# Gated attention and MLP at decode: the Tile kernel rewritten with its own semaphores, and TensorE's rounds 0 to 11 as three loops

## The chip, the cores and the metric

The kernel runs on one core of one Trainium2 chip. A core has five engines that run side by side, each with an instruction stream of its own: TensorE (PE, matrix products; its weight loads are listed as PEld), VectorE (DVE), ScalarE (ACT), GpSimd (POOL) and SyncE (SP, which here only issues transfers). [...] Sixteen DMA engines carry data between HBM and the on-chip memory (SBUF); every transfer is cut into packets that are shared out among them. Matrix products land in PSUM, eight banks of 128 partitions by 512 float32 values.

The metric is the device time of one execution in microseconds (us). Before the change it is 680.88 us, the median of three runs (680.88 to 681.34).

## The reference

One token for each of two sequences (B = 2, D = 448) goes through an attention block with a cache (16 heads, 4096 cached positions, 256 values a head) and through a small MLP (F = 1792); a gate mixes the two. All is float32.

```
q      = (x @ wq) split into 16 heads of 256
scores = q . k_cache / 16          # 2 x 16 x 4096
p      = softmax(scores)
a      = (p . v_cache) @ wo
r      = max(x @ w1 + b1, 0)
b      = (r * r) @ w2 + b2
g      = sigmoid(sum(x * gate_w))
out    = g * a + (1 - g) * b       # 2 x 1 x 448
```

`k_cache` and `v_cache` have 2 x 16 x 4096 x 256 float32 values each, 134.2 MB each. Every one of them is read once.

## The kernel before

**Rounds.** The work goes in 16 rounds. Round i is one pair of heads of one sequence: `rounds[i] = (b, n)`, heads 2n and 2n+1, b alternating. A round has a K tile and a V tile, each 128 partitions by 64 rows of 256 values (8.4 MB): partitions 0 to 63 hold one head's 4096 positions, 64 to 127 the other's. There are three such buffers: `kp[0]` and `kp[1]` for K in even and odd rounds, and one, `vp`, for V.

**What a round does.** DVE multiplies the K tile in place by the query (`times_q`, line 282, in two halves) and sums each row (`row_sums`, line 288), which gives the scores. The maximum over partitions goes over PE: DVE reduces (`m`, line 292), PE spreads the column with the identity into `mt` (line 296), DVE reduces again (`nb`, line 302). ACT writes the exponentials as a weight tile `pw` for PE (line 307) with the row sums in `rs`. PE then runs `values` (line 333): 32 products of 16 weight columns by 512 values of V, which accumulate in a PSUM bank, `po_buf`. The 16 columns stand for the 8 (head, sequence) pairs of a group of four heads, so that a group's four rounds add into the same bank; columns that are not this round's have to be zero. Two weight tiles, `pw0` and `pw1`, are used in turn (by b), and DVE clears one with a memset where a tile passes to other columns (line 434). Two banks, `po_buf0` and `po_buf1`, are used in turn by group.

**The end of a group.** Rounds 0 to 3, 4 to 7 and 8 to 11 are the wide groups. After the fourth round's `softmax`, `sums` (line 313, PE) and `norm` (lines 319 to 322, DVE) give the normalised, gated reciprocals `rl`. After its `values`, `take_turn` transposes the accumulated bank: ACT copies it in four pieces into `shared` (line 350), PE multiplies them with `rl` into `ot` (line 355, 16 products), ACT copies `ot` to `oT` (line 360). The group's `wo` block (1.8 MB) is loaded into `kp[0]` once DVE has finished the first half of the next round's K there (`load_wo`, line 112), and `project` (line 374, 8 products of 448 columns) adds the group's output to `acc`. Only then may the K tile of a later round overwrite `kp[0]`. Rounds 12 to 15 form two narrow groups and the end: V of round 14 goes into a K buffer, V of round 15 comes in five parts, `wo` and `w2` follow, and `late` (line 379) adds all to `fin`.

**Loads.** All large transfers are issued by SP on one queue, in the order of the program: `wq`, K0, `w1`, K1, then V and K in turn: V(i), K(i+2). Each waits for the buffer to be free: V(i+1) for `values` of round i on PE, K(i+2) for the `row_sums` of round i on DVE, and the K after a group also for `project` on PE. The queue takes an issue before the one ahead has landed, so a load that is issued early enough leaves the DMA engines no gap.

**What sets the order.** Each engine runs its instructions in the order in which the code writes them (the Tile context schedules nothing). Tile adds the semaphores, a PSUM or SBUF buffer for each name, and at its end a wait for everything and two barriers over all engines.

## Time and profile before

| | |
|---|---|
| median of three runs | 680.88 us (680.88 to 681.34) |
| span of the profiled execution, first to last instruction | 678.9 us |
| what the median has beside that span | 2.0 us |
| bytes read from HBM | 289.56 MB, 427 GB/s over the span |
| DVE busy | 573.2 us (84%) |
| PE busy | 245.9 us (36%) |
| ACT busy | 35.5 us (5%) |

The profiled execution's time outside its span isn't listed; the 2.0 us are the difference between the median and the span. "Busy" is the time in which an engine had an instruction in work; register, branch and semaphore instructions are not counted. A line such as "DVE kp L282 <- DMA kp<-in_A_k_cache_dram: 53.2" says that DVE stood idle ahead of its line 282 for 53.2 us in all, until a transfer of K landed. "DMA share" in a table of windows is the mean busy share of the sixteen DMA engines in that stretch (packets that overlap an edge can push it over 1). The rows that carry the argument stand in the prediction.

### The profile page before, as it was taken

The numbers are of one execution on the slowest core, as the hardware profiler recorded it, in microseconds if no ns is written. First come the engines' busy times: TensorE is split into PE (matmuls) and PEld (weight loads), VectorE is DVE, ScalarE is ACT, GpSimd is POOL, SyncE is SP. The second block draws the span as 40 slices with busy tenths as digits, with TensorE's granted clock in tenths as the row PEclk, the third lists the DMA queues.
The fourth block names the chain that finished last, engine by engine and source line by source line (L and its number), as shares of the span: only waits on it lengthen the run. The fifth ranks groups of instructions, "written<-read, shape, count | busy, mean of one in ns | idle before, by whom it ended". The sixth has DMA issues, their size and how long they took to land.

```text
span 678.9 us, 3814 instructions
## 1 busy us (share of the span) xinstructions
PE 245.9 (36%) x1658; PEld 78.9 (12%) x1658; DVE 573.2 (84%) x150; ACT 35.5 (5%) x116; POOL 0.7 (0%) x6
## 2 busy tenths in 40 slices
PE   2522250503308541240515644050512550602476
PEld 1100210100104110010101301010100310100122
DVE  3069999999899995979989895998989799999920
ACT  0001000000001000000000100000000200100000
POOL 0000000000000000000000000000000000000000
PEclk9956575665757656575856578575655775755789
DMA  9999999999999999999999999999999999999996
GB/s 379 440 421 441 440 430 444 432 440 437 429 436 407 452 432 432 432 433 432 432 430 432 436 432 433 432 437 432 432 432 432 412 458 413 426 456 432 399 423 267
DMA packets 7628, 289.80 MB, mean 427 GB/s; under 512 B 950, under 2 KB 1084, under 8 KB 2364
## 3 DMA queue, kind: packets, MB, share of 16 engines
q1 hardware_dynamic: 7448, 289.54, 98.9%
q8 instruction: 13, 0.21, 0.1%
q10 hardware_dynamic: 164, 0.02, 0.0%
q14 instruction: 3, 0.02, 0.0%
HBM read 289.56 MB, written 0.00 MB: 427 GB/s over the span
## 4 chain that ended last, share of the span: by engine, by line
DVE 47%; DMA 44%; issue 6%; PE 3%; ACT 0%; SPq 0%; DVEq 0%; ACTq 0%
DMA kp<-in_A_k_cache_dram 32%; DVE kp L282 25%; DVE s L288 21%; DMA vp<-in_A_v_cache_dram 9%; DMA kp<-in_B_w_dram 2%; PE po_buf L333 2%; PE mt L296 0%; DVE pw L434 0%; PE fin L379 0%; ACT pw L307 0%; DVE m L292 0%; PE sum L313 0%; DVE nb L302 0%; SPq L77 0%; DVE hb L270 0%
## 5 line engine op out<-in xcount | busy, mean ns | idle before, releaser
L282 DVE TENSOR_TENSOR kp<-kp,q 128x8192 f32<-128x8192 f32 (+2 forms) x34 | 278.2, 8182 | 53.2 <-DMA kp<-in_A_k_cache_dram 53.2
L288 DVE TENSOR_REDUCE s<-kp 128x32 f32<-128x8192 f32 x32 | 277.9, 8686 | 1.1
L333 PE MATMUL po_buf<-vp,pw 128*16 128x512 f32 (+1 forms) x960 | 140.9, 747 | 219.1 <-DMA vp<-in_A_v_cache_dram 219.1
L333 PEld LDWEIGHTS po_buf<-vp,pw 128*16 128x16 f32 (+1 forms) x960 | 31.0, 112 | 324.2 <-issue 248.3
L296 PE MATMUL mt<-ident,m 128*64 128x64 f32 x64 | 7.3, 317 | 138.9 <-DVE m L292 138.9
L374 PE MATMUL acc<-kp,oT 128*2 128x448 f32 x48 | 26.8, 730 | 18.8 <-issue 18.8
L307 ACT ACTIVATE pw<-s,nb 64x64 f32<-64x64 f32 x32 | 11.1, 347 | 388.6 <-DVE nb L302 388.4
L296 PEld LDWEIGHTS mt<-ident,m 128*64 128x64 f32 x64 | 4.8, 192 | 149.6 <-issue 127.6
L355 PE MATMUL ot<-rl,shared 128*128 128x8 f32 x96 | 17.0, 307 | 3.8 <-ACT shared L350 3.4
L355 PEld LDWEIGHTS ot<-rl,shared 128*128 128x128 f32 x96 | 16.1, 253 | 7.2 <-ACT shared L350 7.2
L238 PE MATMUL pq<-qs,ident 128*64 128x256 f32 x64 | 14.1, 529 | 0.7 <-ACT qs L226 0.7
L200 PE MATMUL ph<-vp,xT 128*4 128x448 f32 x28 | 7.2, 679 | 17.3 <-DMA vp<-in_B_w_dram 17.3
L333 PE MATMUL po_buf<-kp,pw 128*8 128x512 f32 x64 | 9.6, 752 | 8.7 <-DMA kp<-in_A_v_cache_dram 8.7
L302 DVE TENSOR_REDUCE nb<-mt 128x1 f32<-128x64 f32 x16 | 3.6, 224 | 10.7 <-PE mt L296 10.7
L350 ACT ACTIVATE shared<-po_buf 128x512 f32<-128x512 f32 x12 | 6.5, 594 | 86.5 <-PE po_buf L333 81.1
L200 PE MATMUL po_buf<-vp,xT 128*4 128x512 f32 x56 | 7.8, 714 | 4.9 <-DMA vp<-in_A_wq_dram 4.9
L241 ACT ACTIVATE q<-pq 128x256 f32<-128x256 f32 x16 | 6.1, 383 | 62.5 <-PE pq L238 62.3
L374 PEld LDWEIGHTS acc<-kp,oT 128*2 128x2 f32 x48 | 4.8, 103 | 38.9 <-issue 38.9
L319 DVE RECIPROCAL rc<-sum 128x8 f32<-128x8 f32 (+1 forms) x5 | 1.0, 196 | 9.2 <-PE sum L313 9.2
L307 ACT ACTIVATION_READ_ACCUMULATOR pw<-s,nb 64x1 f32 x32 | 5.9, 184 | 0.0
L434 DVE MEMSET pw<- 128x512 f32 x10 | 4.8, 485 | 0.6
L238 PEld LDWEIGHTS pq<-qs,ident 128*64 128x64 f32 x64 | 4.4, 176 | 4.2 <-issue 2.3
(61 smaller groups left out, 58.1 us busy)
## 6 DMA issues: line engine op xcount, KB each, us to landing
kp<-in_A_k_cache_dram SPq DMA_DIRECT2D x4, 4096.0 KB, 27.6
vp<-in_A_wq_dram SPq DMA_DIRECT2D x1, 7168.0 KB, 19.5
kp<-in_A_wo_dram SPq DMA_DIRECT2D x4, 1792.0 KB, 25.5
vp<-in_A_v_cache_dram SPq DMA_DIRECT2D x1, 4096.0 KB
vp<-in_B_w_dram SPq DMA_DIRECT2D x1, 3136.0 KB
vp<-in_A_v_cache_dram SPq DMA_DIRECT2D x1, 2048.0 KB, 30.7
kp<-in_B_w_dram SPq DMA_DIRECT2D x2, 896.0 KB, 27.4
vp<-in_A_v_cache_dram SPq DMA_DIRECT2D x1, 1024.0 KB
```

Of the source, the lines that this page charges most:

```text
L200: nc.tensor.matmul(out[32 * g:32 * g + 2 * B, :width], xT[:, half, c].rearrange("p s b -> p (s b)"), t[:, (a * n + g) * width:(a * n + g + ...
L238: nc.tensor.matmul(pq[k * PH:(k + 1) * PH, :DH], ident[:, r:r + 1].to_broadcast([P, PH]), qs[:, k * DH:(k + 1) * DH], start=True, stop=True)
L241: nc.scalar.activation(q_sb[i], pq[:, :DH], AF.Copy)
L282: nc.vector.tensor_tensor(kt, kt, q_sb[i].unsqueeze(1).to_broadcast([P, hi - lo, DH]), op=ALU.mult)
L288: nc.vector.tensor_reduce(s_t[i][:, at], rows(kp[i % 2])[:, at, :], axis=AX.X, op=ALU.add)
L296: nc.tensor.matmul(mt[at, :PH], m.to_broadcast([P, PH]), ident[:, at], start=True, stop=True)
L307: nc.scalar.activation(pw[b][at, :, 2 * c:2 * c + 2], s_t[i][at].rearrange("p (m s) -> p m s", s=2), AF.Exp, bias=nb[at], accum_out=rs_t[u ...
L333: nc.tensor.matmul(po[r:r + 4 * n, :], pw[b][:, m, :4 * n], vt[:, 2 * m:2 * m + 2, :].rearrange("p j d -> p (j d)"), start=(k == 0 and b = ...
L350: nc.scalar.activation(o_w[:, s], pv[:, s, lo:lo + nj // 2].unsqueeze(2).to_broadcast([P, nj // 2, HG, HP]), AF.Copy)
L355: nc.tensor.matmul(ptv[:, lo + j, :], ov[:, s, j, :], rl_t[u][:, :, s], start=(s == 0), stop=(s == 1))
L374: nc.tensor.matmul(acc[:, :D], oT[g][:, j, :], wo_sb[g][:, j, :], start=False, stop=(g == NG - 2 and j == HJ - 1))
L434: nc.vector.memset(pw[b], 0.0)
```

## The change

The kernel is written without Tile. A small recorder, `Flow`, takes every operation with the regions that it reads and writes, works out which waits are needed, and emits each engine's stream with one semaphore for each engine and one for each transfer's buffer. The arithmetic, the tiles' sizes, the transfers and their order on SP stay.

- PE's rounds 0 to 11 are three loops of four passes (`flow.loop`, `next_pass`, `end_loop`, emitted with `nc.Fori`). The loop's body is `values`, then `mt`, then `pq`, the query of a later round. A looped instruction can't wait for a count that differs from pass to pass, so three hand-overs are tokens: the waiting engine waits for a semaphore's fixed value and takes it off again (`pw` from ACT, `v` from the DMA, `m` from DVE, and `q` from ACT). [...]
- All passes have to name the same operands. So there is one weight tile (`pw0`) and one bank (`po0`) for rounds 0 to 11. After each `values`, ACT overwrites the round's columns with zeros (`clear`), in place of DVE's memsets; after the first and second group ACT zeroes the bank, and every product is issued without a start flag. ACT also copies a column of the identity into `sel` (`pick`) so that `pq` can read the same operand in each pass; the query of round i+3 is made after `mt` of round i+1.
- `sums`, `norm`, the transposition (`turn_wide`) and `project` of a group all stand behind the group's loop on PE, that is, after `mt` of the following round. Before, `sums` and the transposition stood ahead of that `mt`.
- `mt`, `pq` and `sm` have one PSUM bank each.
- At the end SP waits for the two output transfers and clears the semaphores. There is no wait or barrier of the other engines.

TensorE at the end of the first group and in the next round, before the change (line 333 is `values`, 355 the transposition, 374 `project`):

```order
L333 MATMUL po_buf0_85<-vp_71,pw1_94 16x512 x32
L355 MATMUL ot0_446<-rl0_407,shared_135 128x8 x16
L296 MATMUL mt4_482<-ident_78,m4_480 64x64 x2
L374 MATMUL acc_89<-kp0_69,oT0_467 2x448 x8
L238 MATMUL pq6_498<-qs_130,ident_78 64x256 x2
L333 MATMUL po_buf1_87<-vp_71,pw0_92 16x512 x32
```

The same place now; all products have the line of one helper (332), the lines 161 are the loop's own, and the rows from the first `po0` to `COMPARE_AND_BRANCH` run four times:

```order
L161 ISA
L161 UNCONDITIONAL_BRANCH
L332 MATMUL po0<-vp,pw0 16x512 x32
L332 MATMUL mt<-ident,m 64x64 x2
L332 MATMUL pq<-qs,sel 64x256 x2
L161 REGISTER_ALU
L161 COMPARE_AND_BRANCH
L332 MATMUL sm<-rs0,ones_pp 128x8
L332 MATMUL sm<-rl0,shared 128x8 x16
L332 MATMUL acc<-kp0,oTw 2x448 x8
```

The transposition (`sm<-rl0,shared`) has moved from ahead of the next round's `mt` to behind it, directly ahead of `project`, and `sums` (`sm<-rs0,ones_pp`) has come with it.

SP's end before (line 98 loads `w2`, line 500 writes half of the output):

```order
L98 DMA kp_70<-in_B_w_dram 128x896
L98 DMA kp_70<-in_B_w_dram 128x1792 x2
L98 DMA kp_70<-in_B_w_dram 128x1344
L98 DMA kp_70<-in_B_w_dram 128x448
L500 DMA out_dram<-shared 4x112
L524 UNCONDITIONAL_BRANCH
```

And now:

```order
L253 DMA kp<-in_B_w_dram 128x896
L253 DMA kp<-in_B_w_dram 128x1792 x2
L253 DMA kp<-in_B_w_dram 128x1344
L253 DMA kp<-in_B_w_dram 128x448
L253 DMA out_dram<-shared 4x112
L168 ISA
```

The loads stand as before; the branch to Tile's closing block, with its barriers, has become one clearing of the semaphores.

The diff, cut to its core:

```diff
+class Flow:
...
+    def op(self, eng, fn, r=(), w=(), give=None, take=(), dma=None):
...
+        for t in take:
+            p = self.tokens[t].pop(0)
+            o.takes.append((t, 16 if p.proc not in self.eng else 1))
+            self.learn(know, p)
...
+        def one(o):
+            e = self.eng[o.eng]
+            for t, n in o.takes:
+                e.wait_ge(sem(t), n).then_inc(sem(t), -n)
+            for p in o.waits:
+                e.wait_ge(sem(p.proc), counts[id(p)])
+            i = o.fn()
...
+                    passes, body, slot = o
+                    with nc.Fori(0, passes, engines=bass.OrderedEngineSet([TYPES[PE]]),
+                                 head_slot=None if slot is None else {TYPES[PE]: slot}):
+                        for p in body:
+                            one(p)
+            if eng == SP:
...
+                nc.sync.sem_clear(range(nums[0], nums[0] + len(nums)))
...
+    def pick(i):
+        c = col(i)
+        op(ACT, lambda: s_.activation(sel, c, AF.Copy), r=["ident"], w=["sel"], give="q")
...
+    def clear(i):
+        b, n = rounds[i]
+        u, k = unit_of[2 * n]
+        at = pwt[0].rearrange("p m (k b s) -> p m k b s", b=B, s=2)[:, :, k:k + 2, b, :]
+        op(ACT, lambda: s_.activation(at, zero.unsqueeze(2).unsqueeze(3).to_broadcast([P, NK // 2, 2, 2]), AF.Copy), r=["zero"],
...
+    def turn_wide(u):
...
+        if u < NG - 2:
+            op(ACT, lambda: s_.activation(po, zero.to_broadcast([P, 512]), AF.Copy), r=["zero"], w=["po0"])
...
-    for i, (b, n) in enumerate(rounds[:-4]):
...
-        vt = load_v(i, vp)
-        mt = maximum(i)
-        softmax(i, mt)
-        if done:
-            norm(u, sums(u))
...
-        if group is not None:
-            project(group)
...
-        load_k(i + 2)
-        make_q(i + 2)
-        values(i, vt)
-        if done:
-            take_turn(u)
-        rest(i + 1, 0, 0)
...
-                nc.vector.memset(pw[b], 0.0)
-        if done:
-            load_wo(u, i + 1)
-            group = u
+    for i in range(LOOPED):
+        if i % HG == 0:
+            flow.loop()
+        flow.next_pass()
         vt = load_v(i, vp)
+        if i < last - 3 - 1 or i + 2 < 14:
+            load_k(i + 2)
         values(i, vt)
+        clear(i)
         rest(i + 1, 0, 0)
...
+        if i % HG == HG - 1:
+            load_wo(i // HG, i + 1)
+        maximum(i + 1, True)
+        softmax(i + 1)
+        make_q(i + 3, True)
+        if i < LOOPED - 1:
+            pick(i + 4)
+        if i % HG == HG - 1:
+            u = i // HG
+            flow.end_loop(16 * u)
+            sums(u)
+            norm(u)
+            turn_wide(u)
+            project(u)
...
-    nc.sync.dma_start(ov[0], y4[0:P:32, :])
-    nc.scalar.dma_start(ov[1], y4[1:P:32, :])
+    load(SP, "out0", ov[0], y4[0:P:32, :], ["out0"], r=[("shared", 0, DQ)])
+    load(ACT, "out1", ov[1], y4[1:P:32, :], ["out1"], r=[("shared", 0, DQ)])
+    op(SP, lambda: nc.sync.nop(), r=["out0", "out1"])
+    flow.emit()
```

## The prediction

> **What bounds the kernel now.** I read the page from the top: the engines' shares, the DMA rows, the chain, then windows, waits and timelines of the places that the change touches.

> ```profile
> span 678.9 us, 3814 instructions
> PE 245.9 (36%) x1658; PEld 78.9 (12%) x1658; DVE 573.2 (84%) x150; ACT 35.5 (5%) x116; POOL 0.7 (0%) x6
> q1 hardware_dynamic: 7448, 289.54, 98.9%
> q8 instruction: 13, 0.21, 0.1%
> DVE 47%; DMA 44%; issue 6%; PE 3%; ACT 0%; SPq 0%; DVEq 0%; ACTq 0%
> ```

> The chain of waits names DVE first, and DVE is busy for 84%. That misleads. The load queue q1 fills 98.9% of the time of sixteen DMA engines, and a table of windows shows that this has no weak stage:

> ```profile
> core 0: us, PE busy (x) PEld busy (x) DVE busy (x) ACT busy (x) POOL busy (x), PEclk, DMA share, GB/s
> 40.00:640.00 600.00, 206.71 (x1264) 65.63 (x1264) 558.88 (x123) 30.74 (x104) 0.00 (x0) 0.62 1.00 433
> 0.00:40.00 40.00, 12.91 (x76) 4.26 (x76) 5.71 (x23) 2.85 (x5) 0.70 (x6) 0.92 0.97 413
> ```

> From 40 to 640 us the share is 1.00 at 433 GB/s, 27 GB/s for each of the sixteen. The 289.54 MB of q1 at that rate are 668.7 us of the 678.9. DVE's chain runs inside this: a DVE that ends sooner issues the next K sooner, behind loads that are queued already. So the span is the head until the first byte, 668.7 us of transfer, whatever unbalances the sixteen engines, and the tail. In the middle the change can only lose, by letting the queue run dry.

> How the transfers end is seen in windows of half a microsecond:

> ```profile
> 671.00:671.50 0.50, 0.50 (x32) 0.50 (x24) 0.00 (x0) 0.00 (x0) 0.00 (x0) 1.00 1.01 409
> 671.50:672.00 0.50, 0.50 (x31) 0.50 (x26) 0.00 (x0) 0.00 (x0) 0.00 (x0) 1.00 0.82 333
> 672.00:672.50 0.50, 0.46 (x20) 0.19 (x9) 0.00 (x0) 0.00 (x0) 0.00 (x0) 1.00 0.60 240
> 672.50:673.00 0.50, 0.00 (x0) 0.00 (x0) 0.00 (x0) 0.00 (x0) 0.00 (x0) 1.00 0.50 201
> 673.00:673.50 0.50, 0.48 (x21) 0.48 (x25) 0.00 (x0) 0.00 (x0) 0.00 (x0) 1.00 0.43 172
> 673.50:674.00 0.50, 0.47 (x20) 0.20 (x9) 0.00 (x0) 0.00 (x0) 0.00 (x0) 1.00 0.23 93
> 674.00:674.50 0.50, 0.00 (x0) 0.00 (x0) 0.00 (x0) 0.00 (x0) 0.00 (x0) 1.00 0.37 122
> 674.50:675.00 0.50, 0.35 (x16) 0.35 (x20) 0.00 (x0) 0.00 (x0) 0.00 (x0) 1.00 0.05 18
> ```

> The share doesn't drop at once. The first of the sixteen engines are done at 671.5, half of them by 672.5, the last near 674.6, though all had the same bytes of q1. The seven shares from 671.5 on add up to 3.00, times 0.5 us: evenly spread, the work would have ended at 673.0. Something has held some engines back by up to 3.1 us. The candidate is q8: thirteen packets of instructions. 0.21 MB over thirteen is 16 KB each, and over the 3316 instructions of PE and PEld (2 x 1658) 64 bytes each, so q8 is TensorE's code. Its 0.1% (0.05 to 0.15 before rounding) of 16 x 678.9 us is 5.4 to 16.3 us, or 0.42 to 1.25 us a packet, of one engine each time. Thirteen packets can't be even over sixteen engines; an engine that carried two or three of them is late by about what is seen.

> The tail behind the last load, and the closing rows of Tile (line 524):

> ```profile
> 674.65 0.99 PE fin L379 x32
> 675.72 0.26 ACT shared L498
> 676.01 0.65 SPq L500 DMA_DIRECT2D out_dram<-shared  x1
> L524 SPq DRAIN  x3: 7/7/7, 678.2 to 678.5; - x3
> L524 SPq EVENT_SEMAPHORE  x7: 17/28/28, 676.7 to 678.8; - x7
> L524 POOLq EVENT_SEMAPHORE_RANGE_CLEAR  x1: 96/96/96, 678.5 to 678.5; - x1
> ```

> The output is issued at 676.01 and has landed when SP's first drain stands at 678.2; from there to 678.9 are two barriers and a clearing of semaphores.

> **The change part by part.** The sum is made against the profiled span, 678.9, and the 2.0 us by which the median of the runs (680.88) exceeds it are carried over unchanged.

> *End without barriers.* Removed: what lies between 678.2 and 678.9, 0.7 us. Added: SP's own clearing, 0.1 us by the 96 ns row, while five fewer semaphore waits at 28 ns and more are ahead of it, so these cancel. All of it is on the path. Term: -0.7 us (bounds -0.5 and -0.8).

> *Shorter TensorE code.* The program calls 505 products where there were 829, and four instructions stand for each (3316 over 829): 2020 of 64 bytes, 8 packets in place of 13, if a pass through a loop doesn't load its code again. Five packets fewer are 0.1 to 0.4 us on the mean engine, but the end is set by the worst one. If that loses one packet of 1.25 us, the last load lands 1.2 us sooner. Bounds: 0, if the late engines keep their packets; and -2.0, that is 674.6 less 673.0 for perfect balance, and 0.4 for the mean. I take -1.2, the upper price of a packet, since a lag of 3.1 us can't be made of two or three packets of 0.42. Term: -1.2 us.

> *Branches.* Three entries and nine taken returns, with twelve compares, are new on PE. No row shows a PE branch. SP's entry branch lies in the 0.07 us of "issue" ahead of the first load:

> ```profile
> 0.67 0.07 issue
> 0.74 0.39 SPq L77
> ```

> That is the lower bound of one; the upper is a packet of code, 1.25 us, fetched while PE stands. Cover: each return is followed by `values`, which waits for V, in all 219.1 us in 17 waits:

> ```profile
> PE po_buf L333 <- DMA vp<-in_A_v_cache_dram: 219.1, 17, 26.1
> ```

> 12.9 us each on average, so up to there a branch costs nothing. Without the cover it delays V(i+1), which is issued when `values` ends: the issue of V5 at 256.28 (below) came 9.3 us before K6, ahead of it in the queue, had landed for DVE at 265.57. Head: SP loses its entry branch, under 0.07 us. Term: 0.

> *The group's end moved.* This is the one place where something new comes between a computation and an issue. The rows of the first group:

> ```profile
> 212.57 1.08 ACT L350 ACTIVATE shared<-po_buf 128x512 f32<-128x512 f32 x2 [24.62 <-PE po_buf L333]
> 220.06 0.73 ACT L360 ACTIVATE oT<-ot 32x16 f32<-32x16 f32 x4 [3.25 <-PE ot L355]
> 222.16 0.16 DVE L292 TENSOR_REDUCE m<-s 128x1 f32<-128x64 f32 x1
> 222.47 0.48 PE L296 MATMUL mt<-ident,m 128*64 128x64 f32 x4 [2.45 <-DVE m L292]
> 223.96 0.18 ACT L307 ACTIVATION_READ_ACCUMULATOR pw<-s,nb 64x1 f32 x1
> 226.83 8.57 PE L374 MATMUL acc<-kp,oT 128*2 128x448 f32 x16 [3.87 <-issue]
> 235.43 0.33 SPq L127 DMA_DIRECT2D kp<-in_A_k_cache_dram  x1
> 246.23 9.99 PE L333 MATMUL po_buf<-vp,pw 128*16 128x512 f32 x64 [10.24 <-DMA vp<-in_A_v_cache_dram]
> 256.28 0.33 SPq L132 DMA_DIRECT2D vp<-in_A_v_cache_dram  x1
> 265.57 8.69 DVE L282 TENSOR_TENSOR kp<-kp,q 128x8192 f32<-128x8192 f32 x1 [6.35 <-DMA kp<-in_A_k_cache_dram]
> ```

> Before, the transposition (212.57 to 220.79, 8.2 us) was over before `m` of round 4; `project` waited for `wo` until 226.8, and K6 was issued at 235.43. Now it starts behind `mt`, the exponentials (over at 224.1), the copy of `pq` and a `pick`, say 224.7, with `sums` and `norm` beside them; with 8.2 us it ends at 232.9, `project` at 241.5, and K6 is issued there, 6.1 us later. V4, ahead of K6 in the queue, is still landing until 246.2 (the `values` that waits for it). 4.7 us of cover remain, and DVE should reach `m` sooner, since `norm` and two memsets are gone from its way. Term: 0; without the cover it costs what goes beyond 246 less about 1 us from issue to first byte (the issue at 0.74 above brings bytes from 1.5 to 2.0 on).

> ```profile
> 1.00:1.50 0.50, 0.00 (x0) 0.00 (x0) 0.40 (x1) 0.00 (x0) 0.29 (x1) 1.00 0.00 0
> 1.50:2.00 0.50, 0.00 (x0) 0.00 (x0) 0.45 (x2) 0.00 (x0) 0.00 (x0) 1.00 3.53 1154
> ```

> *Zeroing on ACT, single buffers.* DVE loses ten memsets (4.8 us busy); nothing is gained, since it then waits longer for K, which is late already:

> ```profile
> L434 DVE MEMSET pw<- 128x512 f32 x10 | 4.8, 485 | 0.6
> DVE kp L282 <- DMA kp<-in_A_k_cache_dram: 53.2, 9, 28.2
> ```

> ACT gains twelve `clear` (128x128 values; about 0.3 us, near the 128x112 copy of 0.26 in the tail's rows), eleven `pick` (0.2, near the 0.73 us for four small copies above) and two zeroings of a bank (0.54, half of the two copies of 1.08), some 7 us beside 35.5. A `clear` stands between `values` of a round and the exponentials of the next; the wait for V covers it. One weight tile and one bank add no wait: `mt` of the next round stands behind `values` in both orders, and the bank is free 13 us before V4 lands.

> Sum: 678.9 - 0.7 - 1.2 = 677.0, with the 2.0 outside 679.0 us.

> **The rivals.**
> *The late engine stays late.* Which engine gets which packet isn't seen in the page; the last could still carry two or three of the eight. Then only the end's 0.7 counts: 680.2 us.

> *Every taken branch loads code again.* [...] No row of this case shows a branch of PE. Worked out here from the rows: twelve more packets, 20 in place of 13, stretch the lag of 3.1 us to 4.8, so that the end comes 1.7 later, less 0.7: 681.9 us. Against it stands that a body is 36 products, 144 instructions, less than one packet of 256. [...]

> *The queue runs dry at a group's end.* If the way from `m` to K6 grows by more than about 3.7 us (4.7 less 1), at the loop's exit above all, the sixteen engines idle for the rest. To lose the 1.9 us gained and 1.4 more it has to grow by 7; by 10 us, eight packets of code in series, the time is 679.0 + 6.3 = 685.3 us. For it speaks that K6 is the tightest issue of the rows above; against it, that the code behind the exit follows in sequence, and that at 433 GB/s a single 8.4 MB load (19.4 us) of cover is only needed three times.

> **How the numbers follow.** Two runs of this kernel tell apart differences of about 0.2%, 1.4 us. Forecast (both gains): 64 in 100, with 678.4 to 679.8 as its own range (both bounds of the end, and 0.6 to 1.7 for the code); about 4 of the 64 lie within 0.2%. Late engine stays: 14. Reloading: 8. Dry queue: 14. So faster 0.60, same 0.26 (4 + 14 + 8), slower 0.14. The predicted time is the forecast's, 679.0. The range runs from 678.2, a little under the forecast's low end for a better balance, to 681.0, which takes in the second case and the milder part of the third.

> **What would show it.** Right: 8 packets in q8; the DMA share still 1.00 from 40 to 640 and falling from 1 to 0 in under 2.5 us; the last load about a microsecond earlier; nothing behind SP's output but one clearing, with 2.2 us from issue to end; K6 issued near 241 with the share unbroken. Wrong: q8 at 13 or more packets, or a share below 1 behind a group's end. DVE's waits for K should grow by about the memsets' 4.8 us without any effect on the end.

## The result and the profile after

The changed kernel takes 678.52 us (median of 5 runs, 678.43 to 678.64); the kernel before, on the same chip, 680.88 (5 runs, 680.70 to 681.34). The ratio is 0.9963, with an interval of 0.9951 to 0.9975: faster by 0.37%, 2.4 us. In the profiled runs it is 678.43 us with a span of 677.1, against 680.88 with 678.9. So 1.8 us went inside the span, and some 0.65 around it: in these two runs 1.3 us lie outside the span now (678.43 less 677.1), 2.0 before (680.88 less 678.9).

From the page of the changed kernel, its head, the engines, the queues and the chain:

```profile
span 677.1 us, 3790 instructions
PE 246.3 (36%) x1658; PEld 83.3 (12%) x1658; DVE 569.6 (84%) x141; ACT 42.6 (6%) x142; POOL 0.7 (0%) x6
q1 hardware_dynamic: 7448, 289.54, 99.2%
q8 instruction: 8, 0.13, 0.1%
DVE 41%; DMA 36%; PE 0%; issue 0%; ACT 0%; DVEq 0%
```

The load queue carries the same bytes at a slightly higher share. TensorE's code has come down from thirteen packets to eight, though PE executes the same 1658 products. DVE lost 3.6 us of work and ACT gained 7.1.

The windows of the changed kernel, with the columns of the prediction's tables (DMA share and GB/s last): the middle of the program, then half microseconds at its end.

```profile
40.00:640.00 600.00, 207.92 (x1264) 70.45 (x1264) 557.16 (x113) 37.81 (x130) 0.00 (x0) 0.62 1.00 433
...
671.50:672.00 0.50, 0.00 (x0) 0.00 (x0) 0.00 (x0) 0.00 (x0) 0.00 (x0) 1.00 0.90 341
672.00:672.50 0.50, 0.41 (x20) 0.41 (x24) 0.00 (x0) 0.00 (x0) 0.00 (x0) 1.00 0.52 208
672.50:673.00 0.50, 0.50 (x24) 0.27 (x12) 0.00 (x0) 0.00 (x0) 0.00 (x0) 1.00 0.44 172
673.00:673.50 0.50, 0.04 (x4) 0.00 (x0) 0.00 (x0) 0.00 (x0) 0.00 (x0) 1.00 0.14 54
673.50:674.00 0.50, 0.29 (x13) 0.29 (x17) 0.00 (x0) 0.00 (x0) 0.00 (x0) 1.00 0.03 11
```

Up to 640 us nothing has changed: share 1.00 at 433 GB/s in both kernels. At the end the shares from 671.5 on add up to 2.03, where they were 3.00: half a microsecond of all sixteen engines' time less. The last bytes come before 674, not near 674.6.

The last rows of the timeline, and the row of the closing clear:

```profile
673.80 0.85 PE L332 MATMUL fin<-kp,hT 128*2 128x112 f32 x28
674.72 0.26 ACT L657 ACTIVATE shared<-fin 128x112 f32<-128x112 f32 x1 [5.03 <-PE fin L332]
675.01 0.64 SPq L253 DMA_DIRECT2D out_dram<-shared  x1
L168 SPq EVENT_SEMAPHORE_RANGE_CLEAR  x1: 88/88/88, 677.0 to 677.0; - x1
```

The output is issued at 675.01 instead of 676.01, and from there to the end of the span are 2.1 us instead of 2.9. So of 2.45 us between the two profiled runs 1.0 is an earlier last load, 0.8 a shorter end, and 0.65 lies outside the span.

The first group's end in the changed kernel (timeline; start, duration, engine, line):

```profile
218.51 0.22 DVE L420 TENSOR_REDUCE m<-s 128x1 f32<-128x64 f32 x1
...
221.07 1.07 ACT L488 ACTIVATE shared<-po 128x512 f32<-128x512 f32 x2
...
222.28 3.55 PE L332 MATMUL sm<-rl,shared 128*128 128x8 f32 x16 [1.54 <-ACT shared L488]
...
227.07 3.58 PE L332 MATMUL sm<-rl,shared 128*128 128x8 f32 x16 [1.23 <-ACT shared L488]
...
230.68 0.74 ACT L497 ACTIVATE oTw<-sm 32x16 f32<-32x16 f32 x4 [3.04 <-PE sm L332]
...
231.47 8.04 PE L332 MATMUL acc<-kp,oTw 128*2 128x448 f32 x16 [0.82 <-ACT oTw L497]
239.60 0.33 SPq L253 DMA_DIRECT2D kp<-in_A_k_cache_dram  x1
...
246.34 1.06 PE L332 MATMUL po<-vp,pw 128*16 128x512 f32 x4 [6.83 <-PEq L145]
```

From `m` to K6 it now takes 21.1 us, where it was 13.3 (222.16 to 235.43), but `m` itself comes 3.65 us sooner. K6 goes out 4.2 us later than before and the share above is unbroken.

The remaining rows on which the verdicts below rest: PE's branches (nanoseconds, shortest, median, longest), DVE's waits for K, and the new `clear` on ACT.

```profile
L161 PEldq COMPARE_BRANCH  x15: 76/208/309, 77.9 to 537.6; - x15
DVE kp L403 <- DMA kp<-in_A_k_cache_dram: 57.3, 10, 28.2
L449 ACT ACTIVATE pw<-zero 128x128 f32<-128x128 f32 x12 | 3.7, 311 | 326.9 <-PE po L332 326.9
```

### The profile page after: what moved, and what is told of

It reads as the page before. It is cut to its first block, busy times and chain, and to the rows that moved or that the text cites. A ratio compares the mean times of both kernels' runs of the same rounds, so it can differ in the third digit from the quotient of the medians.

```text
span 677.1 us, 3790 instructions
## 1 busy us (share of the span) xinstructions
PE 246.3 (36%) x1658; PEld 83.3 (12%) x1658; DVE 569.6 (84%) x141; ACT 42.6 (6%) x142; POOL 0.7 (0%) x6
## 3 DMA queue, kind: packets, MB, share of 16 engines
q1 hardware_dynamic: 7448, 289.54, 99.2%
## 4 chain that ended last, share of the span: by engine, by line
DVE 41%; DMA 36%; PE 0%; issue 0%; ACT 0%; DVEq 0%
DMA kp<-in_A_k_cache_dram 32%; DVE s L408 21%; DVE kp L403 20%; DMA kp<-in_B_w_dram 4%; PE fin L332 0%; PE mt L332 0%; DVE nb L430 0%; ACT shared L657 0%; DVE rc L460 0%; DVE rl L461 0%; DVE rc L459 0%; DVE m L420 0%; DVEq L147 0%
## 5 line engine op out<-in xcount | busy, mean ns | idle before, releaser
L403 DVE TENSOR_TENSOR kp<-kp,q 128x8192 f32<-128x8192 f32 (+2 forms) x34 | 278.2, 8182 | 57.3 <-DMA kp<-in_A_k_cache_dram 57.3
L332 PE MATMUL po<-vp,pw 128*16 128x512 f32 (+1 forms) x960 | 138.8, 736 | 223.9 <-PEq L145 207.1
L332 PEld LDWEIGHTS po<-vp,pw 128*16 128x16 f32 (+1 forms) x960 | 31.1, 111 | 327.4 <-issue 306.4
L332 PE MATMUL sm<-rl,shared 128*128 128x8 f32 (+1 forms) x112 | 23.6, 347 | 9.1 <-ACT shared L488 8.1
L332 PE MATMUL acc<-kp,oTw 128*2 128x448 f32 x48 | 24.3, 673 | 2.5 <-ACT oTw L497 2.5
L332 PEld LDWEIGHTS sm<-rl,shared 128*128 128x128 f32 x112 | 23.0, 311 | 10.7 <-DVE rl L461 4.6
L332 PE MATMUL po<-kp,pw 128*8 128x512 f32 x64 | 10.1, 790 | 8.1 <-DMA kp<-in_A_v_cache_dram 8.1
L332 PE MATMUL pq<-qs,sel 128*64 128x256 f32 x48 | 12.3, 594 | 0.0
L332 PE MATMUL po<-vp,xT 128*4 128x512 f32 x56 | 7.7, 711 | 4.9 <-DMA vp<-in_A_wq_dram 4.9
L488 ACT ACTIVATE shared<-po 128x512 f32<-128x512 f32 x12 | 6.5, 591 | 11.4 <-PE sm L332 11.4
L379 ACT ACTIVATE q<-pq 128x256 f32<-128x256 f32 x16 | 6.1, 384 | 13.1 <-PE pq L332 12.8
L332 PEld LDWEIGHTS acc<-kp,oTw 128*2 128x2 f32 x48 | 4.5, 98 | 20.1 <-issue 17.3
```

What stands on the lines that cost most here:

```text
L332: i = t_.matmul(out_, lhsT, rhs, start=start, stop=stop, skip_group_check=True)
L379: op(ACT, lambda: s_.activation(t, pq[:, :DH], AF.Copy), r=["pq"], w=[f"q{i % 3}"])
L403: vec(lambda: v_.tensor_tensor(kt, kt, q.unsqueeze(1).to_broadcast([P, hi - lo, DH]), op=ALU.mult), at + [f"q{i % 3}"], at)
L488: op(ACT, lambda s=s, lo=lo: s_.activation(o_w[:, s], pv[:, s, lo:lo + HJ // 2].unsqueeze(2).to_broadcast([P, HJ // 2, HG, HP]), AF.Copy), ...
```

## The experiments

Three questions: is it the number of code packets that sets the last load's time; is it the missing barriers that the rest comes from, inside the span or outside it; and how near was the group's end to letting the queue run dry? All edits are made to the changed kernel (two of them to the one with its loops written out). None leaves work out; the products, copies and memsets that some add have results that nobody reads.

| run | us, median (range) | ratio to before | q8 packets | output issued |
|---|---|---|---|---|
| before | 680.88 (680.70 to 681.34) | 1 | 13 | 676.01 |
| the change | 678.52 (678.43 to 678.64) | 0.9963 [0.9951, 0.9975] | 8 | 675.01 |
| unroll | 679.66 (679.36 to 679.91) | 0.9982 [0.9973, 0.9991] | 13 | 676.08 |
| code9 | 679.50 (679.18 to 679.79) | 0.9978 [0.9969, 0.9987] | 11 | 676.14 |
| code18 | 681.00 (680.55 to 681.12) | 1.0001 [0.9992, 1.0010] | 18 | 677.70 |
| more_loop | 683.21 (682.19 to 683.70) | 1.0030 [1.0019, 1.0042] | 11 | 679.88 |
| more_unroll | 684.19 (683.44 to 684.45) | 1.0047 [1.0034, 1.0061] | 18 | 680.78 |
| end_barrier | 679.08 (678.95 to 679.23) | 0.9972 [0.9963, 0.9982] | 8 | 675.08 |
| tile_end | 679.29 (679.09 to 679.51) | 0.9976 [0.9967, 0.9985] | 8 | 675.01 |
| pe_waits | 678.78 (678.41 to 678.98) | 0.9966 [0.9952, 0.9980] | 8 | 674.85 |
| act_waits | 678.55 (678.31 to 678.69) | 0.9964 [0.9950, 0.9978] | 8 | 674.76 |
| dve_load | 678.31 (678.18 to 678.79) | 0.9962 [0.9949, 0.9975] | 8 | 675.31 |
| late8 | 678.61 (678.51 to 680.01) | 0.9968 [0.9956, 0.9981] | 8 | 676.36 |
| late18 | 689.34 (688.64 to 689.45) | 1.0123 [1.0106, 1.0140] | 8 | 685.24 |

### The loops written out

The same instructions in the same order, with the four passes of each loop written one behind the other.

```diff
-                    with nc.Fori(0, passes, engines=bass.OrderedEngineSet([TYPES[PE]]),
-                                 head_slot=None if slot is None else {TYPES[PE]: slot}):
+                    for _ in range(passes):
                         for p in body:
                             one(p)
```

> The changed kernel with its three loops written out: the same products, one weight tile, one bank, the same end, but TensorE's code of 3375 instructions instead of 2058. Theory (code packets hold single DMA engines back): 13 packets in q8 again, the DMA share runs out from 671.5 to 674.6 as before the change, the output is issued about 1.0 us later than 675.0, 679.5 us in all. Rival (the last load came earlier because DVE lost its memsets or because waits are fewer): 8 or 13 packets make no difference, 678.5 us.

679.66 us, 1.1 above the change; the kernel before took 680.85 beside it and 680.88 beside the change. From its page, its windows and its timeline:

```profile
q8 instruction: 13, 0.21, 0.1%
...
674.00:674.50 0.50, 0.11 (x7) 0.00 (x0) 0.00 (x0) 0.00 (x0) 0.00 (x0) 1.00 0.38 126
674.50:675.00 0.50, 0.22 (x12) 0.23 (x16) 0.00 (x0) 0.00 (x0) 0.00 (x0) 1.00 0.08 29
...
676.08 0.64 SPq L252 DMA_DIRECT2D out_dram<-shared  x1
```

Thirteen packets are back, and with them the late end: engines still move data after 674.5, as before the change, and the output goes out 1.07 us later than with loops. This one edit gives back the whole gain at the last load, and nothing of the end.

The records of the single packets in the trace say how. A code packet of 16 KB takes about 1.05 us (0.92 to 1.12 in the kernel before and in the change), and the load's packet of 64 KB behind it takes 2.89 to 2.97 us instead of 2.42. The records don't name the engine, but the sixteen parts of each load keep their distances from load to load until a code packet comes; from then on one part lands about 1.55 us later than it did, against the others (1.3 to 1.6 in most cases of the kernel before and of the change). Of the last big load the sixteen parts land over 3.2 us before (671.96 to 675.16), over 3.3 when the loops are written out, over 2.2 with them (672.01 to 674.21). Before, each of the first eight packets delayed another part, and the ninth to the twelfth delayed parts that had been delayed once. The four parts that were delayed twice land last, 3.0 to 3.2 us behind the first. In the change no part is delayed twice; the part that lands last lay 0.8 us behind the first before its code packet came and 2.3 us behind it afterwards, so the end moved by 1.0 and not by 1.55. The other queue of instructions, q14, has three packets of 8 KB in the span before and two in the change, which shift a part by 0.6 to 1.0 us; with the loops written out there are two as well, so they don't explain the difference.

By the page of the change eight packets hold 0.13 MB, 16 KB each: 256 instructions, at the 64 bytes worked out in the prediction. TensorE doesn't stand for its code as far as the rows show, none of which has it waiting for code. The loads do pay for it: thirteen packets in place of eight delay the last of them by 1.07 us.

### More code

27 products of 4 columns each per pass, with results that nobody reads, in loops and written out. In the first pair they stand behind `pq` (`ph` and `ident` as in the listing):

```diff
         make_q(i + 3, True)
+        op(PE, mms([(ph[:PH, :2 * B], ident[:2 * B, :PH], ident[:2 * B, :2 * B], True, True)
+                    for _ in range(27)]), r=["ident"], w=["ph"])
```

> The loops written out, and 27 idle products of 64x4 added to each of the twelve passes (their results go to a bank that nobody reads): 4671 instructions, 18 packets. Theory: if the packets come round to the same engines after eight, the last load is 1.3 us later than with 13 packets, 680.8 us; if they are spread evenly, 0.4 us later, 679.9. Rival (TensorE's work doesn't matter and code neither): 678.5 us.

> The same 27 idle products in each pass, but in the loops: the same extra work for TensorE, 2382 instructions, 9 packets, and a body of some 258 instructions, more than one packet. Theory: 9 packets, within 0.5 us of the changed kernel, 678.5 to 679.0 us. Rival (the extra work itself costs): as late as with the loops written out. Rival (a body of more than a packet is loaded again on each return): 16 packets or more, 680 us or later.

Both missed by 3 to 5 us, 684.19 and 683.21. The place was badly chosen: the products stand ahead of `sums` at each group's end, take 5.9 us there and push K6 back. The row of K6 and two windows of the looped one, and then the same windows of the change:

```profile
244.55 0.33 SPq L253 DMA_DIRECT2D kp<-in_A_k_cache_dram  x1
...
240.00:245.00 5.00, 4.46 (x12) 0.85 (x10) 5.00 (x2) 0.00 (x0) 0.00 (x0) 1.00 0.66 279
245.00:250.00 5.00, 3.45 (x20) 0.84 (x24) 5.00 (x1) 0.00 (x0) 0.00 (x0) 0.66 1.11 419
```

```profile
240.00:245.00 5.00, 0.00 (x0) 0.00 (x0) 5.00 (x1) 0.00 (x0) 0.00 (x0) 0.71 0.97 419
245.00:250.00 5.00, 3.66 (x20) 0.95 (x24) 4.97 (x2) 0.00 (x0) 0.00 (x0) 0.50 1.00 433
...
400.00:410.00 10.00, 4.56 (x28) 1.14 (x32) 9.96 (x2) 0.00 (x0) 0.00 (x0) 0.66 0.98 426
410.00:420.00 10.00, 5.25 (x52) 1.41 (x44) 6.84 (x3) 1.77 (x7) 0.00 (x0) 0.98 1.04 452
```

The share falls to 0.66 where the change has 0.97. This pair says nothing on code, then, but it shows the rival of the dry queue at work: K6 five microseconds later (244.55 against 239.60) costs about 1.0 us at the first group's end (0.31 less 0.11, times 5).

In the second pair the same products stand ahead of `values`, where PE waits for V anyway.

```diff
             load_k(i + 2)
+        op(PE, mms([(ph[:PH, :2 * B], ident[:2 * B, :PH], ident[:2 * B, :2 * B], True, True)
+                    for _ in range(27)]), r=["ident"], w=["ph"])
         values(i, vt)
```

> The changed kernel with 27 idle products of 64x4 in each looped pass, this time ahead of `values`, where TensorE waits for V anyway (their results go to a bank that nobody reads). A body of some 258 instructions, 9 packets of code by its length. Theory: the work is covered, 9 to 11 packets, 678.5 to 679.2 us. Rival (TensorE's extra work itself costs time): as late as code18.

> The same with the loops written out: 4671 instructions, 18 packets, the same work for TensorE. Theory: as late as `unroll` or later, 679.6 to 680.9 us; the upper end if a 17th packet falls on an engine that has had two and that before 670 us. Rival: no later than code9.

Equal work on PE, and 679.50 in loops against 681.00 written out. K6 is issued at 240.72 and 239.32, so the queue is not the cause. The code queue's row of the looped one, then that of the one written out with two windows of its end:

```profile
q8 instruction: 11, 0.18, 0.1%
```

```profile
q8 instruction: 18, 0.29, 0.2%
...
675.00:676.00 1.00, 0.71 (x32) 0.44 (x20) 0.00 (x0) 0.00 (x0) 0.00 (x0) 1.00 0.06 25
676.00:677.00 1.00, 0.61 (x28) 0.55 (x32) 0.00 (x0) 0.00 (x0) 0.00 (x0) 1.00 0.03 11
```

With eighteen packets one engine is still at work after 676, and the parts of the last big load land over 4.9 us. That fits; the time is 0.1 us above the upper end of what was expected. The looped one is 0.3 us over its expectation, and its row says why: by its length it has nine packets (2382 instructions, as counted for the first pair, at 256 a packet), and eleven were fetched. The extra products bring a body to about 258 instructions, just over the 256 of a packet, but the returns didn't fetch more here: in the packets' records none follows one of the nine returns within 43 us. Of the three that the change doesn't have, one comes 1.9 us ahead of a return (415.3), and two come 7.6 us behind the exits of loops (227.1 and 386.1). In the looped run of the first pair, which fetched eleven as well, three come 1.6 to 2.7 us behind returns (155.2, 270.5 and 430.4). What a body over one packet fetches, and why the place of the products matters, stays open. With eight, eleven, thirteen and eighteen packets the output goes out at 675.01, 676.14, 676.08 and 677.70: not in proportion to their number, but in steps of 1.1 and 1.6 us, about one packet on the last engine.

### The end

A barrier of all engines behind SP's clear; and, closer to the kernel before, a barrier, GpSimd's clear and a second barrier.

```diff
     flow.emit()
+    nc.all_engine_barrier()
```

> The changed kernel with one barrier over all engines behind SP's clearing. Theory (engines that end early do their share of what follows the kernel while SP still waits for the output): the span grows by the barrier's 0.3 to 0.5 us, and the time outside the span goes back from 1.35 to 2.0 us: 679.4 to 679.7 us. Rival (what lies outside the span is fixed, and differs for another reason): 678.8 to 679.0 us.

```diff
-                nc.sync.sem_clear(range(nums[0], nums[0] + len(nums)))
+                self.nums = range(nums[0], nums[0] + len(nums))
...
     flow.emit()
+    nc.all_engine_barrier()
+    nc.gpsimd.sem_clear(flow.nums)
+    nc.all_engine_barrier()
```

> The changed kernel with Tile's whole ending: a barrier over all engines, the clearing on GpSimd, a second barrier. Theory: the span grows by 0.7 us and the time outside it goes back from 1.35 to 2.0 us: 679.7 to 679.9 us. Rival (the time outside the span is not the barriers' doing): span 677.8, 679.1 to 679.3 us.

Two barriers with the clear cost 0.77 us by the medians, one 0.56. In both the output is issued at 675.0 or 675.1, as in the change. From the page of the one with two barriers:

```profile
span 677.7 us, 3812 instructions
...
L664 POOLq EVENT_SEMAPHORE_RANGE_CLEAR  x1: 228/228/228, 677.2 to 677.2; - x1
```

Its profiled run took 679.51, so 0.6 us are back inside the span (677.7 against 677.1) and 0.5 outside it (1.8 against 1.3). With one barrier the span grows by 0.3 (677.4), and outside it is 1.8 as well (679.23). Both totals are below what the theory gave (679.4 and 679.7 us at the least). The second even lies in the range of its rival, but its parts don't: it is the time outside the span that came back. The theory expected 2.0 there, and that figure was too high from the start. In the 67 runs of the kernel before that were timed beside these experiments, the time less the span is 1.81 us at the median (1.75 to 1.96); in the five runs of the change it is 1.33 to 1.42. So the barriers bring back all of what lay outside. The time around the span is no constant of the kernel here: it was about 0.45 us shorter where the engines other than SP didn't wait for the last transfer. Inside the span 0.2 of the kernel before's end was not reproduced.

Which engine is it? In two runs one engine alone waits for a word that SP gives behind the landing of the output:

```diff
+    over = nc.alloc_semaphore("s_over")
+    nc.sync.nop().then_inc(over, 1)
+    nc.tensor.wait_ge(over, 1).then_inc(over, -1)
```

(`nc.scalar` in the other.)

> The changed kernel, with TensorE alone waiting for a word from SP behind its clearing. Where the 0.5 us outside the span come from: if TensorE's own ending is the long one, the time outside the span grows from 1.3 to 1.8 us and the whole to about 679.1; if it is another engine's, or takes several engines, 678.6 us.

> The same with ScalarE alone waiting. If ScalarE's own ending is the long one, 679.1 us with 1.8 outside the span; else 678.6 us.

678.78 and 678.55, where 679.1 was expected of the engine that does it alone. By these medians ACT's wait costs nothing, and PE's 0.26 is inside the scatter of its own runs (678.41 to 678.98). The time less the span scatters less and says more: 1.58 to 1.69 us in the five runs with PE waiting, 1.49 to 1.55 with ACT, against 1.33 to 1.42 in the change and 1.75 to 1.83 with one barrier. But the kernel with eight idle copies below, whose end is that of the change, has 1.47 to 1.61. So neither engine alone brings all of it back; PE may bring back a part, and for ACT nothing is shown. DVE, GpSimd and combinations were not tried, and it stays open.

### Vector engine

Eight memsets in each of six rounds, about 2 us of DVE work ahead of `maximum`.

```diff
+        for _ in range(8 if i in (5, 6, 7, 9, 10, 11) else 0):
+            fill("pw1", pwt[1])
         vec(lambda: v_.tensor_reduce(m, s, axis=AX.X, op=ALU.max), ...
```

> Eight memsets of a weight tile that isn't in use, about 2 us, ahead of `m` in six rounds (5, 6, 7, 9, 10, 11): DVE gets 12 us more work where it waits for K. Theory (the load queue is the bound): 678.4 to 678.8 us, and DVE's waits for K shrink by as much. Rival (DVE, first in the chain of waits, sets the time): 688 us or more.

678.31 us. The engines' row of its page and DVE's wait for K:

```profile
PE 249.3 (37%) x1658; PEld 83.8 (12%) x1658; DVE 581.9 (86%) x189; ACT 42.5 (6%) x142; POOL 0.7 (0%) x6
...
DVE kp L403 <- DMA kp<-in_A_k_cache_dram: 40.5, 7, 28.1
```

12.3 us more work, 16.8 us less waiting for K, no loss. The engine that the chain names first is not the bound here.

### How late K6 may go out

8 and 18 idle copies on ACT ahead of each of the group's ends, on the way from `m` to K6.

```diff
+        for _ in range(8):
+            op(ACT, lambda: s_.activation(ph, zero.to_broadcast([P, 512]), AF.Copy), r=["zero"], w=["ph"])
         if u < NG - 2:
```

> The changed kernel with eight idle copies of 0.59 us on ACT in the transposition of each group; five are covered by products that ACT waits for, so `project` and the K behind it come 1.8 us later (K6 at 241.4 instead of 239.6). Theory (the engines have V4 until 246, and a new load needs some 2 us to its first bytes): no loss, 678.5 to 678.9 us. Rival (each microsecond at a group's end is on the path): three groups, 5 us, 684 us.

> The same with eighteen copies: 7.7 us later at each group's end, K6 at 247.3, K10 at 407.1. Theory (the queue runs dry past a point near 242.5 for K6 and 401.5 for K10, and not at all for the third group, where V12 lands at 574): 4.7 and 5.5 us, 688 to 689.5 us. Rival of all three groups on the path: 23 us, 701 us; rival of a queue that never runs dry: 678.5 us.

With eight copies the median is 678.61. K6's row and the window around it:

```profile
241.68 0.33 SPq L253 DMA_DIRECT2D kp<-in_A_k_cache_dram  x1
...
240.00:250.00 10.00, 5.10 (x25) 1.07 (x27) 9.96 (x2) 0.00 (x0) 0.00 (x0) 0.72 1.00 419
```

2 us later than in the change, and no gap. Two of its six runs, the profiled one among them, took 680.0 and 679.9. In the profiled one the fourth code packet, at 397.8, delayed a part that had been delayed before, and the parts of the last big load land over 3.3 us; the other has no trace. The output goes out 1.35 us later than in the change (676.36), again about one packet on the last engine, with eight packets as there.

With eighteen copies the time is 689.34, K6 goes out at 248.20, and the queue runs dry at two of the group's ends:

```profile
248.20 0.33 SPq L253 DMA_DIRECT2D kp<-in_A_k_cache_dram  x1
...
240.00:245.00 5.00, 5.00 (x9) 0.91 (x8) 5.00 (x1) 0.00 (x0) 0.00 (x0) 0.56 0.62 265
245.00:250.00 5.00, 5.00 (x35) 1.52 (x37) 4.96 (x2) 0.00 (x0) 0.00 (x0) 1.00 0.60 210
...
400.00:410.00 10.00, 6.74 (x12) 1.27 (x13) 10.00 (x2) 3.08 (x9) 0.00 (x0) 0.59 0.73 316
410.00:420.00 10.00, 8.75 (x70) 2.06 (x67) 9.96 (x2) 0.31 (x1) 0.00 (x0) 1.00 0.79 315
```

Against the change's four windows above, the shares lost are 0.35 and 0.40 of 5 us and 0.25 and 0.25 of 10: 3.75 and 5.0 us. Together that is 8.75 of the 10.2 us by which the span grew (687.3 against 677.1). K6's first packet starts at 249.16, 1.0 us behind its issue, not the 2 us of the expectation, which no run shows. If each microsecond past the latest harmless issue of K6 costs one, two estimates of it follow: 248.2 less 3.75 is 244.5, and 244.55 less the 1.0 of the looped run with idle products is 243.5. So by these estimates the change has about 4 to 5 us to spare at 239.6; what is measured is no loss at 241.7.

None of these kernels beats the change by more than the scatter of the runs.

## Why the prediction was right

679.0 was predicted, 678.52 measured, for the mechanisms named: what bounds the kernel is the sixteen DMA engines' work (share 1.00 from 40 to 640 us) and the lag of the last of them (3.1 us before), not DVE, to which 12.3 us of work were added without a loss. Step by step:

- *End without barriers, -0.7:* measured -0.8 inside the span (2.9 to 2.1 us behind the output's issue), at the upper bound. The two barriers put back gave 0.6 of it.
- *Shorter TensorE code, -1.2:* eight packets, as counted, and -1.0 at the output's issue; by itself, from the loops written out, -1.07 there and -1.14 in the medians. The choice between the bounds (one packet less on the worst engine) was right in kind, and the lag of 3.1 us before is two packets on one engine. The size was partly luck: a packet costs its engine about 1.55 us (1.05 of its own, 0.5 for the load's packet behind it), not 1.25, and the end moved by less than that because the engine that is last now lay 0.8 us behind before its packet came. The rival *the late engine stays late* fell for this kernel, though a run can still meet it: of the six runs with eight copies the profiled one did, and a second took as long.
- *The time outside the span, carried over at 2.0:* this is the term that was mis-sized. It measured 1.33, and a barrier of all engines brought 1.8 back. The 2.0 came from one run and was itself 0.2 above the median of 67 others (1.81); the other 0.45 us are an effect of the change. The page doesn't show this time, and the forecast treated it as independent of the change. With it corrected the sum would have been 678.3 (677.0 and 1.33), against 678.43 in the profiled run.
- *Branches, 0:* 0.08 to 0.31 us each by their row; no packet beyond the eight. The rival *every taken branch loads code again* fell: behind the nine returns of the change, with a body of 144 instructions, no packet came within 50 us. With a body of about 258 at most three of the nine returns can have fetched one (the looped run of the first pair). No row here shows PE standing for a packet behind a branch: the longest branch took 0.31 us in the change and 0.32 with a body of about 258. No run shows the twelve packets of which that rival's 681.9 us are made; the change fetched eight in all.
- *The group's end moved, 0:* right in its effect, with K6 at 239.6 instead of 241.5. Two errors cancelled in part. The way from `m` to K6 took 21.1 us, not the 19.3 assumed (222.16 to 241.5). The transposition was mis-sized: from its first copy (221.07, 2.6 us behind `m`, as assumed) to the end of `oTw` (231.4) it takes 10.35 us, not 8.2, since PE now starts its products 1.2 us behind the first copy instead of 0.65 and ACT's second pair of copies waits 3.8 us for products instead of 2.1; `project` is 0.5 us shorter. But `m` came 3.65 us sooner, which the forecast named without counting it. The cover ends, by estimate, at 243.5 to 244.5, not at 245. The rival *the queue runs dry* is real, and is 4 to 5 us away.
- *Zeroing on ACT, 0:* a `clear` takes 0.31 us, ACT gained 7.1 us, and DVE waits 4.1 us more for K (57.3 against 53.2), close to the memsets' 4.8 that it lost.

## What to carry to other kernels

When the share of the DMA engines is 1.00 through the program, look at how the sixteen end, in windows of half a microsecond, and count the code packets: most of them delayed one of the sixteen parts of a load by 1.3 to 1.6 us here, and the parts delayed twice landed last in the kernel before. Loops with a body of 144 instructions removed five of thirteen here; with a body of about 258, eleven were fetched where the same code written out had eighteen. What loops move to their exit must not push the next load's issue past the point where the queue runs dry: K6 2.1 us later left no gap here (share 1.00), and 8.6 us later it cost 3.75 us. Drop barriers behind the last store (one cost 0.56 us here, two with the clear 0.77), and don't expect the time outside the span to stay as it was (1.33 to 1.42 us in the change, 1.75 to 1.83 with one barrier).
